# A fused attention and two-expert-layer kernel: first loads in a fixed order, and eight unread products ahead of the first round in place of eighteen in three places

## The chip, the core and the metric

The kernel runs on one core of a Trainium2 chip. The metric is the device time of one execution in microseconds (us). A core has a matrix engine (TensorE, PE in the rows), three engines for elementwise work (VectorE = DVE, ScalarE = ACT, GpSimd = POOL) and SyncE (SP), which here only issues DMA transfers. Each engine works through its own list of instructions; semaphores make one engine wait for another or for a transfer.

## The reference

Three stages follow each other on 2,304 tokens (4 batches of 576) with 512 channels:

```
q_p, k_p = exp(h - max h), h = x*scale @ omega.T - |x*scale|^2/2     # 8 heads of 64, 128 features
num = q_p @ (k_p.T @ v);  den = q_p @ sum(k_p) + 1e-6;  x = num/den   # linear attention
x = (silu(xn @ w_gate) * (xn @ w_val)) @ w_out                        # xn: RMS norm, 1536 wide
out = experts(x)   # 8 experts of 1024; each token goes to one, picked greedily, 288 tokens each
```

The weights of the middle stage are in float64 on the host and reach the kernel as pairs of 32-bit words.

## The kernel before, in words

**Attention** is a list of items: for batch 0 ten key items (head pair `p` 0 to 3, two or three groups `g` each), then eight query items, and so on for the other batches. An item's first step on PE is the projection (`proj_whole`, L393, tile `pp`); then DVE takes the maximum over the features (L397, `mx`) and ACT the exponential of four heads' columns (L400, `ft`, four instructions). One tick later PE multiplies the features of a key item with the values (L440, or L443 for the rest of a batch, tile `pm`). So in a tick PE runs the projection of one item and then the value products of the item before it; this is called a round below. `pp` has two buffers: a projection can start when ACT has read the `pp` of two items earlier.

**Weight units** run beside this. A unit loads 512 KB of word pairs into `ws` (L567, three buffers), ACT makes the magnitude (L572, tile `dw`), DVE the word (L576 to L578), ACT and GpSimd the split into two parts (L601, L602). The middle layer's products (L660 to L663, tile `gv`) enter PE's order from tick 23 and need these weights and the attention's output.

**Batch 1 and later** split their keys: ACT copies the high part (`split_k`, L365, `kh` from `kt`), GpSimd takes the low part (L366). The first such item comes after the eight query items of batch 0.

**What sets the order.** PE's order is written by hand (`manual_schedule` over the ticks). ACT, DVE, GpSimd and, before the change, SP get their order from a scheduler that works from its own picture of when each instruction is ready; whatever it decides is fixed in the program, and the engine then waits at each instruction in turn. Before the change, constants (`cf`, which holds the identity for the transposes, L779) were issued first of all by SP. A transfer on SP also waits until the transfer eight places earlier has landed, since eight semaphores (DMAHW0 to DMAHW7) are used in turn.

**Unread products.** `warm(n)` (L789) issues n products of a zeroed tile into a PSUM tile `lg` that nothing reads: 10 ahead of the first tick, 4 behind tick 0 and 4 behind tick 1.

Of the kernel before, what the change touches and what calls it, by code (L numbers as in the profile page):

```python
# [291 lines left out]
def kernel(ctx, tc, qT, kT, kC, v1, vC, om, wgv, rms, wo, woT, wg2, w1, w2, cfd, trd, cid, out, dbg=None):  # L292
    nc = tc.nc
# [10 lines left out]
    cf = keep.tile([128, C_N], F32, name="cf")  # L304
    ident = cf[:, C_ID:C_SL]
    cs = keep.tile([128, 1], F32, name="cs")
    gr = keep.tile([128, DM], F32, name="gr")
# [9 lines left out]
    wg2s = keep.tile([128, KD, E], F32, name="wg2s")  # L317
# [17 lines left out]
    def load_k(b, p):  # L335
        if b == 0:

            room = wpool.tile([128, 2, 1024], F32, name="wc")
            rooms[p] = room
            kt = room[:, 0, :512]  # L340
            vt = room[:, 1, :8 * (D + 1)].rearrange("p (t h d) -> p t h d", t=4, h=2)
        else:
            kt = kq.tile([128, 512], F32, name="kt", bufs=3)
            vt = kq.tile([128, 4, 2, D + 1], F32, name="vt", bufs=3)
        nc.sync.dma_start(kt, kT[b, p])
        nc.sync.dma_start(vt, v1[b, p])
        kts[b, p], vts[b, p] = kt, vt

    def load_c(b, r):
        if b == 0:  # L350
            kt = rooms[2 * r + 1][:, 0, 512:640]
            vt = rooms[2 * r + 1][:, 1, 520:520 + 4 * (D + 1)].rearrange("p (h d) -> p h d", h=2)
        else:
            kt = kq.tile([128, 128], F32, name="ktc", bufs=1)
            vt = kq.tile([128, 2, 2 * (D + 1)], F32, name="vtc", bufs=1)
        nc.sync.dma_start(kt, kC[b, r])
        nc.sync.dma_start(vt, vC[b, r])
        ktc[b, r], vtc[b, r] = kt, vt
# [10 lines left out]
    def load_q(c):  # L369
        if c < 4:  # L370
            if c == 0:
                st["qroom"] = wpool.tile([128, 4, 4, 128], F32, name="wc")
            qt = st["qroom"][:, c]
        else:
            qt = kq.tile([128, 4, 128], F32, name="qt")
        nc.sync.dma_start(qt, qT[c])
        qhs[c] = qt
# [377 lines left out]
    useq = [WgvUnit(f, g) for f in range(KF) for g in range(2)] + [WoTUnit(f) for f in range(KF)]  # L755
# [6 lines left out]
    nc.gpsimd.memset(idle.bitcast(F32), 0.0)  # L762
    ws = stage.tile([128, 2 * M], F32, name="ws")
    nc.scalar.dma_start(ws, om)
    load_k(0, 0)
    oms = wpool.tile([128, 2 * M], F32, name="wc")
    nc.scalar.mul(oms, ws, SCALE)
    nc.scalar.copy(omh, oms)
    nc.vector.tensor_sub(oml, oms, omh)
    load_k(0, 1)  # L770
    useq[0].load()
    load_k(0, 2)
    useq[1].load()
    load_c(0, 0)
    load_k(0, 3)
    load_c(0, 1)
    for c in range(2):
        load_q(c)
    nc.sync.dma_start(cf, cfd)  # L779
    useq[2].load()  # L780
    nc.sync.dma_start(gr, rms)
    for c in range(2, 4):
        load_q(c)
    nc.sync.dma_start(wg2s, wg2)
    nc.vector.memset(cs, -0.5)

    sink = psL.tile([128, 512], F32, name="lg")
# [1 line left out]
    def warm(n):  # L789
        for _ in range(n):  # L790
            nc.tensor.matmul(sink, idle[:, :128], idle[:, 128:], start=True, stop=True)
# [21 lines left out]
    def run_tick(tick):  # L813
        live = [(lag, items[tick - lag]) for lag in range(NLAG) if 0 <= tick - lag < len(items)]
        conv_pe(PACE[0] if tick < FFN_AT else PACE[1] if conv["next"] < 2 * KF else PACE[2])
        with tc.high_priority(offset=AHEAD_A):
            for lag, it in live:
                it.pe(lag)
        ffn_step_pe()
        for lag, it in live:  # L820
            if lag == 5 and isinstance(it, QItem) and it.hf and it.c * 128 // BLK not in xblk:
                while len(xblk) > 1:
                    ffn_step_el()
                    if not ffn_step_pe():
                        conv_el()
                        conv_pe(1)
        with tc.high_priority(offset=AHEAD_A):
            for lag, it in live:
                it.el(lag)
            if tick + 1 < len(items):  # L830
                items[tick + 1].split()
        ffn_step_el()
        conv_el()
        if tick + AHEAD < len(items):
            items[tick + AHEAD].load()
        if tick >= FFN_AT:
            conv["step"] += STEP - 1
            if conv["step"] >= 1:
                conv["step"] -= 1
                ffn_step_pe()  # L840
                ffn_step_el()

    with tc.manual_schedule(engines={mybir.EngineType.PE}):
        warm(10)
        for tick in range(len(items) + NLAG - 1):
            run_tick(tick)
            if tick < 2:
                warm(4)
    ac.close()


# [367 lines left out]
```

## Time and profile before

| | |
|---|---|
| median of 3 runs | 916.79 us (915.77 to 917.20) |
| the profiled execution | 915.83 us, span 914.0 us |
| PE busy | 898.2 us, 98% of the span |
| DVE busy | 553.6 us, 61% |
| ACT busy | 372.4 us, 41% |

The span runs from the first to the last instruction; 1.8 us of the execution's time lie around it. PE's busy time counts a matrix product from its start to a modelled end, so a busy PE is not a PE at its peak, and the shares are means over stages with different limits.

### The profile page before, as it was taken

Reading aid. Unit: us, or ns where it says so; the run is one execution under the profiler, and the core shown is the slowest. Engines: PE = TensorE matmul, PEld = TensorE weight load, DVE = VectorE, ACT = ScalarE, POOL = GpSimd, SP = SyncE. Lnnn points to the kernel's source line nnn. Section 1 sums busy time; section 2 is a strip of 40 time slices with the busy share of each in tenths; the row PEclk is TensorE's granted clock in tenths of the full one; section 3 lists DMA queues with packets and bytes.
Section 4 is the critical chain, followed back from the end, with each engine's and each line's share of the span. In section 5 each row is a group of like instructions: output and inputs, shape, how many; then the busy total and the mean of one; then the engine's idle time right before and its main releaser. Section 6 shows DMA issues by size and latency. Waiting matters only on the chain.

```text
span 914.0 us, 16175 instructions
## 1 busy us (share of the span) xinstructions
PE 898.2 (98%) x6171; PEld 781.0 (85%) x6171; DVE 553.6 (61%) x1262; ACT 372.4 (41%) x843; POOL 227.3 (25%) x298
## 2 busy tenths in 40 slices
PE   9999999999999999999999999999999999999996
PEld 8788888888888888777798777777789999999995
DVE  4898885656667765322273666666654665556561
ACT  6886565434544554332251110000014544454541
POOL 1354452222224332364241000000021122222111
PEclk9999999999999999999999999999999999999998
DMA  8656453454444642286583767766614656666650
GB/s 300 203 144 218 142 164 116 127 178 128 145 159 161 201 150 81 98 311 248 171 250 142 205 192 213 207 197 199 187 63 125 190 182 203 185 206 195 181 163 26
DMA packets 113213, 158.88 MB, mean 174 GB/s; under 512 B 6640, under 2 KB 70768, under 8 KB 113136
## 3 DMA queue, kind: packets, MB, share of 16 engines
q1 hardware_dynamic: 107328, 143.57, 50.5%
q0 software_dynamic: 3072, 9.44, 3.4%
q10 hardware_dynamic: 2736, 4.85, 1.4%
q8 instruction: 48, 0.79, 0.4%
q14 instruction: 29, 0.24, 0.1%
HBM read 113.79 MB, written 44.04 MB: 173 GB/s over the span
## 4 chain that ended last, share of the span: by engine, by line
PE 85%; issue 7%; DVE 4%; POOL 2%; ACT 2%; DMA 0%; POOLq 0%; ACTq 0%; DVEq 0%
PE py L973 16%; PE gv L660 11%; PE gv L661 10%; PE gv L663 10%; PE ph L1087 3%; PE ph L1084 3%; PE ph L1085 3%; PE py L1095 3%; PE py L1096 3%; PE py L1097 3%; PE pm L497 3%; PE pm L440 2%; PE cnt L181 2%; PE pm L486 1%; PE pp L388 1%
## 5 line engine op out<-in xcount | busy, mean ns | idle before, releaser
L660 PE MATMUL gv<-xh,wc 128*128 128x512 f32 (+1 forms) x480 | 180.0, 381 | 0.7 <-DVE th L673 0.7
L661 PE MATMUL gv<-xh,wc 128*128 128x512 f32 (+1 forms) x480 | 174.3, 370 | 0.0
L973 PE MATMUL py<-wc,ht 128*128 128x512 f32 x648 | 167.1, 404 | 0.0
L973 PEld LDWEIGHTS py<-wc,ht 128*128 128x128 f32 x648 | 114.9, 189 | 19.0
L663 PE MATMUL gv<-xl,wc 128*128 128x512 f32 (+1 forms) x480 | 118.4, 369 | 0.0
L660 PEld LDWEIGHTS gv<-xh,wc 128*128 128x128 f32 x480 | 90.6, 189 | 17.3 <-DVE th L673 1.7
L661 PEld LDWEIGHTS gv<-xh,wc 128*128 128x128 f32 x480 | 90.6, 189 | 13.8
L663 PEld LDWEIGHTS gv<-xl,wc 128*128 128x128 f32 x480 | 85.3, 189 | 15.8
L400 ACT ACTIVATE ft<-pp,mx 128x128 f32<-128x128 f32 x288 | 82.6, 373 | 27.7 <-DVE mx L397 25.0
L673 DVE SCALAR_TENSOR_TENSOR th<-th,gv 128x512 f32<-128x512 f32 (+1 forms) x60 | 37.9, 632 | 84.2 <-ACT th L672 84.2
L688 POOL TENSOR_TENSOR hp<-th,hp 128x512 fp32r<-128x512 f32 (+1 forms) x48 | 60.2, 1254 | 110.1 <-ACT hp L687 97.8
L944 DVE TENSOR_TENSOR wc<-ws,wc 128x512 fp32r<-128x512 f32 x128 | 84.8, 683 | 0.0
L1095 PE MATMUL py<-ehh,wc 128*128 128x288 f32 x256 | 77.7, 304 | 0.0
L1096 PE MATMUL py<-ehl,wc 128*128 128x288 f32 x256 | 75.9, 297 | 0.0
L1097 PE MATMUL py<-ehh,wc 128*128 128x288 f32 x256 | 75.8, 296 | 0.0
L1084 PE MATMUL ph<-exh,wc 128*128 128x288 f32 x256 | 71.6, 302 | 0.0
L1085 PE MATMUL ph<-exh,wc 128*128 128x288 f32 x256 | 69.8, 295 | 0.0
L984 ACT COPY ys<-py 128x512 f32<-128x512 f32 x18 | 10.6, 587 | 144.6 <-PE py L973 103.7
L954 ACT CAST wc<-ws 128x1024 fp32r<-128x1024 f32 x64 | 66.9, 1046 | 2.4 <-ACT ys L984 2.4
L397 DVE TENSOR_REDUCE mx<-pp 128x4 f32<-128x512 f32 (+1 forms) x76 | 50.0, 658 | 14.5 <-PE pp L393 8.1
L672 ACT ACTIVATE th<-gv 128x512 f32<-128x512 f32 (+1 forms) x60 | 33.2, 553 | 61.1 <-PE gv L663 53.3
L1089 DVE SCALAR_TENSOR_TENSOR ehl<-ph,ehh 128x288 fp32r<-128x288 f32 x64 | 29.3, 458 | 46.8 <-ACT ehh L1088 46.8
(214 smaller groups left out, 1714.2 us busy)
## 6 DMA issues: line engine op xcount, KB each, us to landing
ws<-in_w_dram SPq DMA_DIRECT2D x64, 512.0 KB, 4.2
ht<-h_dr SPq DMA_DIRECT2D x54, 512.0 KB, 4.2
h_dr<-hp SPq DMA_DIRECT2D x36, 512.0 KB, 2.8
ws<-in_wgv_dram SPq DMA_DIRECT2D x24, 512.0 KB, 4.3
h_dr<-hp SPq DMA_DIRECT2D x24, 256.0 KB, 2.7
ws<-in_woT_dram SPq DMA_DIRECT2D x12, 512.0 KB, 3.6
ws<-in_wo_dram SPq DMA_DIRECT2D x12, 512.0 KB, 3.8
h_dr<-ht SPq DMA_DIRECT2D x12, 512.0 KB, 3.2
```

The source lines that it names most:

```text
L400: st["ex"] = nc.scalar.activation(ft[:n, g], pp[:n, g], AF.Exp, bias=mx[:n, g:g + 1])
L660: nc.tensor.matmul(pg[:, :n], w[:, 0, v, k], xh[:, k, :n], start=(k == 0), stop=False)
L661: nc.tensor.matmul(pg[:, :n], w[:, 1, v, k], xh[:, k, :n], start=False, stop=False)
L663: nc.tensor.matmul(pg[:, :n], w[:, 0, v, k], xl[:, k, :n], start=False, stop=(k == KD - 1))
L944: nc.vector.tensor_sub(w[:, 1, h], sv[:, h], w[:, 0, h])
L954: nc.scalar.copy(w[:, 0], sv)
L973: nc.tensor.matmul(py, ht[:, i4, a], w[:, l, f % 2], start=(f == 0 and n == 0), stop=(f == KF - 1 and n == 2))
L1084: nc.tensor.matmul(ph, w[:, 0, k, m], xh[:, k], start=(k == 0), stop=False)
L1085: nc.tensor.matmul(ph, w[:, 1, k, m], xh[:, k], start=False, stop=False)
L1095: nc.tensor.matmul(py, w[:, 0, k], hh[:, k], start=(k == 0), stop=False)
L1096: nc.tensor.matmul(py, w[:, 0, k], hl[:, k], start=False, stop=False)
L1097: nc.tensor.matmul(py, w[:, 1, k], hh[:, k], start=False, stop=(k == KE - 1))
```

## The change

The first loads are written in one place, ahead of the preparation of omega, and a manual schedule over SP keeps them in that order: keys and values of head pairs 0 and 1, a weight unit, the rest of batch 0's keys for pairs 0 and 1, pair 2, a weight unit, pair 3 and its rest, two query blocks, then the constants, and so on. The unread products become 8 ahead of the first tick and none behind ticks 0 and 1.

```diff
     nc.scalar.dma_start(ws, om)
-    load_k(0, 0)
+    with tc.manual_schedule(engines={mybir.EngineType.SP}):
+        load_k(0, 0)
+        load_k(0, 1)
+        useq[0].load()
+        load_c(0, 0)
+        load_k(0, 2)
+        useq[1].load()
+        load_k(0, 3)
+        load_c(0, 1)
+        for c in range(2):
+            load_q(c)
+        nc.sync.dma_start(cf, cfd)
+        useq[2].load()
+        nc.sync.dma_start(gr, rms)
+        for c in range(2, 4):
+            load_q(c)
+        nc.sync.dma_start(wg2s, wg2)
     oms = wpool.tile([128, 2 * M], F32, name="wc")
...
-    load_k(0, 1)
-    useq[0].load()
-    load_k(0, 2)
-    useq[1].load()
-    load_c(0, 0)
-    load_k(0, 3)
-    load_c(0, 1)
...
-    nc.sync.dma_start(cf, cfd)
...
-        warm(10)
+        warm(8)
         for tick in range(len(items) + NLAG - 1):
             run_tick(tick)
-            if tick < 2:
-                warm(4)
```

The change moves instructions on SP, ACT, DVE and GpSimd, since the scheduler decides anew behind it. On SP, from the 14th load to the first loads of batch 1 (`kt`, `vt`), before; DMAHW names the semaphore of the transfer eight places earlier:

```order
L357 DMA wc_114<-in_vC_dram 128x260 [waits DMAHW3_49]
L345 DMA wc_126<-in_kT_dram 128x512 [waits DMAHW4_49]
...
L784 DMA wg2s_81<-in_wg2_dram 128x32 [waits DMAHW6_49]
L567 DMA ws_207<-in_wgv_dram 128x1024 [waits DMAHW7_49,DVE_49,Activation_49]
L567 DMA ws_242<-in_wgv_dram 128x1024 [waits DMAHW0_49,DVE_49,Activation_49]
L345 DMA kt_506<-in_kT_dram 128x512 [waits DMAHW1_49]
L567 DMA ws_280<-in_wgv_dram 128x1024 [waits DMAHW2_49,DVE_49,Activation_49]
```

The same place of SP's order in the changed kernel:

```order
L376 DMA wc_129<-in_qT_dram 128x512 [waits DMAHW7_49]
L376 DMA wc_129<-in_qT_dram 128x512 [waits DMAHW0_49]
L776 DMA cf_69<-in_cf_dram 128x339 [waits DMAHW1_49]
L567 DMA ws_133<-in_wgv_dram 128x1024 [waits DMAHW2_49,Activation_49]
L778 DMA gr_71<-in_rms_dram 128x512 [waits DMAHW3_49]
L376 DMA wc_129<-in_qT_dram 128x512 [waits DMAHW4_49]
L376 DMA wc_129<-in_qT_dram 128x512 [waits DMAHW5_49]
L781 DMA wg2s_81<-in_wg2_dram 128x32 [waits DMAHW6_49]
L345 DMA kt_499<-in_kT_dram 128x512 [waits DMAHW7_49]
L346 DMA vt_500<-in_v1_dram 128x520 [waits DMAHW0_49]
```

The first batch-1 key load (`kt_506` before, `kt_499` now) moved ahead of two weight units and stands directly behind `wg2s`; the 22 SP loads ahead of it are the same ones as the 22 that end with `wg2s` before.

On ACT, the third and fourth items of attention before (`ft_199`, `ft_218`), which the unit's magnitude (`dw`) precedes:

```order
L572 ACTIVATE dw_184<-ws_117 128x512 [waits DMAHW4_49]
L400 ACTIVATE ft_199<-pp_190,mx_197 128x128 [waits DVE_49]
L400 ACTIVATE ft_199<-pp_190,mx_197 128x128 x3
L400 ACTIVATE ft_218<-pp_209,mx_216 128x128 [waits DVE_49,Activation_49]
L400 ACTIVATE ft_218<-pp_209,mx_216 128x128 x3
L400 ACTIVATE ft_236<-pp_228,mx_234 128x128 [waits DVE_49]
```

And in the changed kernel (`ft_192`, `ft_211`):

```order
L572 ACTIVATE dw_181<-ws_115 128x512 [waits DMAHW5_49]
L400 ACTIVATE ft_192<-pp_183,mx_190 128x128 [waits DVE_49]
L400 ACTIVATE ft_192<-pp_183,mx_190 128x128 x3
L365 CAST kh_576<-kt_499 128x256 [waits DMAHW7_49]
L365 CAST kh_631<-kt_499 128x256
L400 ACTIVATE ft_211<-pp_202,mx_209 128x128 [waits DVE_49,Activation_49]
L400 ACTIVATE ft_211<-pp_202,mx_209 128x128 x2
L400 ACTIVATE ft_229<-pp_221,mx_227 128x128 [waits DVE_49]
```

Two copies of batch 1's keys (L365, from `kt_499`) now stand between the third and the fourth item; before, they stand behind the second query block's first copy.

On PE, the first rounds before:

```order
L791 MATMUL lg_142<-wc_103 128x512 x9
L393 MATMUL pp_155<-wc_110,wc_107 128x256 [waits DMAHW2_49,Activation_49]
L393 MATMUL pp_155<-wc_110,wc_107 128x256
L791 MATMUL lg_142<-wc_103 128x512 x4
L393 MATMUL pp_169<-wc_110,wc_107 128x256 x2
L440 MATMUL pm_172<-wc_107,ft_160 128x65 [waits DMAHW3_49,Activation_49]
L440 MATMUL pm_172<-wc_107,ft_160 128x65 [waits Activation_49] x3
L791 MATMUL lg_142<-wc_103 128x512 x4
```

And in the changed kernel, through the value products of the fourth item:

```order
L792 MATMUL lg_145<-wc_103 128x512 x7
L393 MATMUL pp_156<-wc_140,wc_109 128x256 [waits DMAHW1_49,Activation_49]
L393 MATMUL pp_156<-wc_140,wc_109 128x256
L393 MATMUL pp_166<-wc_140,wc_109 128x256 x2
...
L393 MATMUL pp_221<-wc_140,wc_112 128x256 [waits DMAHW6_49,DVE_49]
L440 MATMUL pm_169<-wc_112,ft_211 128x65 [waits Activation_49] x4
L393 MATMUL pp_237<-wc_140,wc_119 128x256 [waits DMAHW0_49,DVE_49]
```

The groups of four are gone, and the rest of PE's order is as before: behind the fifth item's projection (`pp_221`) PE waits at `pm_169<-ft_211` for ACT.

## Rows read from the trace of the kernel before

**Rows 1.** The page: span, and each engine's busy time.

```profile
span 914.0 us, 16175 instructions
PE 898.2 (98%) x6171; PEld 781.0 (85%) x6171; DVE 553.6 (61%) x1262; ACT 372.4 (41%) x843; POOL 227.3 (25%) x298
```

**Rows 2.** Windows: stretch, its length, engines' busy us, granted clock, DMA share, GB/s.

```profile
13.50:25.00 11.50, 11.50 (x74) 9.96 (x73) 7.70 (x14) 10.27 (x31) 2.54 (x2) 1.00 0.81 278
25.00:40.00 15.00, 14.22 (x89) 11.27 (x88) 12.37 (x27) 13.07 (x41) 5.98 (x7) 1.00 0.84 261
40.00:60.00 20.00, 17.97 (x135) 16.47 (x135) 17.95 (x36) 18.36 (x55) 10.28 (x14) 1.00 0.38 113
60.00:75.00 15.00, 14.31 (x84) 12.23 (x83) 14.79 (x21) 10.19 (x26) 9.18 (x8) 1.00 0.71 216
75.00:100.00 25.00, 25.00 (x144) 21.74 (x143) 20.38 (x42) 13.85 (x34) 10.04 (x10) 1.00 0.59 175
```

**Rows 3.** Chain that ended last, 0 to 80 us: start, us, what.

```profile
1.43 4.14 PE lg L791 x10
5.57 0.86 PE pp L393 x4
6.43 0.93 PE lg L791 x4
...
9.07 0.98 PE lg L791 x4
10.05 0.87 PE pp L393 x4
10.92 0.84 PE pm L440 x8
...
70.00 0.70 DVE dw L577
```

**Rows 4.** Timeline of ACT and DVE: start, us, what, idle time before it and releaser.

```profile
3.88 0.42 ACT L767 ACTIVATE wc<-ws 128x256 f32<-128x256 f32 x1 [1.41 <-DMA ws<-in_om_dram]
6.47 0.69 DVE L397 TENSOR_REDUCE mx<-pp 128x4 f32<-128x512 f32 x1 [1.28 <-PE pp L393]
8.99 1.14 ACT L400 ACTIVATE ft<-pp,mx 128x128 f32<-128x128 f32 x4 [0.66 <-DVE mx L397]
10.01 0.68 ACT L572 ACTIVATE dw<-ws 128x512 f32<-128x512 f32 x1
13.50 1.69 ACT L400 ACTIVATE ft<-pp,mx 128x128 f32<-128x128 f32 x6 [0.62 <-DVE mx L397]
31.13 0.74 ACT L365 CAST kh<-kt 128x256 fp32r<-128x256 f32 x2
```

**Rows 5.** Timeline of SP's issues, 0 to 20 us.

```profile
1.19 0.42 SPq L345 DMA_DIRECT2D wc<-in_kT_dram  x1
...
2.13 0.43 SPq L567 DMA_DIRECT2D ws<-in_wgv_dram  x1
...
15.13 0.66 SPq L784 DMA_DIRECT2D wg2s<-in_wg_dram  x1
15.90 3.75 SPq L567 DMA_DIRECT2D ws<-in_wgv_dram  x2
```

**Rows 6.** DMA view, windows of rows 5's issues: size, us to landing.

```profile
wc<-in_kT_dram SPq DMA_DIRECT2D x1, 256.0 KB, 3.2
ws<-in_wgv_dram SPq DMA_DIRECT2D x1, 512.0 KB, 6.7
wg2s<-in_wg_dram SPq DMA_DIRECT2D x1, 16.0 KB, 6.4
```

**Rows 7.** DMA view, 0 to 40 us: GB/s in each us.

```profile
GB/s 0 34 224 389 195 185 330 352 398 429 390 393 360 344 261 317 332 311 358 421 260 274 336 119 33 74 233 267 386 141 205 403 248 263 259 230 344 413 352 94
```

**Rows 8.** Windows at the end of the execution, columns as in rows 2.

```profile
904.50:905.00 0.50, 0.50 (x5) 0.29 (x3) 0.14 (x1) 0.03 (x1) 0.00 (x0) 1.00 0.00 0
905.00:909.00 4.00, 0.04 (x1) 0.00 (x0) 1.28 (x4) 0.61 (x2) 2.67 (x5) 1.00 0.28 77
909.00:910.00 1.00, 0.00 (x0) 0.00 (x0) 0.00 (x0) 0.00 (x0) 0.26 (x1) 0.69 0.49 152
910.00:911.00 1.00, 0.00 (x0) 0.00 (x0) 0.00 (x0) 0.00 (x0) 0.00 (x0) 0.50 0.42 131
```

More of the change, by code (lines that the diff above doesn't have):

```diff
@@ L769 @@
     nc.vector.tensor_sub(oml, oms, omh)
-    load_k(0, 1)
-    useq[0].load()
-    load_k(0, 2)
-    useq[1].load()
-    load_c(0, 0)
-    load_k(0, 3)
-    load_c(0, 1)
-    for c in range(2):
-        load_q(c)
-    nc.sync.dma_start(cf, cfd)
[L780 to L784, printed above, removed]
     nc.vector.memset(cs, -0.5)
```

## The prediction, made blind

> **What bounds the kernel now.** I read the page first: PE is busy for 98% of the span [rows 1], but that share hides the start. The chain of waits tells it apart [rows 3]: up to about 24 us it runs over PE alone, round after round, with the unread products in it; after that it changes between ACT, DVE and PE, and at 70 us it still runs over DVE, on the weight units. From 75 us PE is busy in every microsecond [rows 2]. So what the change is worth is decided before 75 us: PE then has a backlog to the end, and a delay (or gain) of ACT and DVE in that stretch is handed on whole. The windows show that little slack is left there: ACT is busy for 10.27 of 11.5 us, 13.07 of 15 and 18.36 of 20 up to 60 us, and DVE for 17.95 of 20 and 14.79 of 15 from 40 to 75 us [rows 2].
>
> **The part that is meant: the unread products.** At the start ten took 4.14 us, 0.41 each; the later groups of four took 0.93 and 0.98, 0.23 to 0.25 each [rows 3]. [...] With eight, the row ends at 1.43 + 8 x 0.41 = 4.7 us. The first projection needs scaled omega, ready at 3.88 + 0.42 = 4.3 us [rows 4], and the first keys, landed at 1.19 + 3.2 = 4.4 us [rows 5, 6] behind the constants, which no longer stand ahead of them. So it starts near 4.8 instead of 5.57 us, 0.8 us earlier. The second projection follows at once (0.86 us each [rows 3]), and the maximum (0.69) and four exponentials (1.14) of item 1 [rows 4] end at 4.8 + 0.86 + 0.69 + 1.14 + 0.1 for the hand-overs = 7.6 us. The value products of item 1 and then the third projection come at about 7.8 us, where before it began at 10.05 [rows 3]: 2.2 us earlier.
>
> **Why this gain isn't kept.** ACT's order in the changed kernel has, behind the third item's exponentials, two copies of batch 1's keys (L365) that read `kt_499`. Nobody needs them for fourteen more items, but ACT takes its list in turn: before, it sat 1.41 us ahead of its first scaling for a transfer while there was nothing else it could do [rows 4]. [...]
>
> *When do they start?* `kt_499` is the 23rd load on SP and stands right behind `wg2s`. The 22 SP loads ahead of it are those of before in another order, so the same bytes have to pass. Before, the last of these was issued at 15.13 us and landed 6.4 us later, at 21.5; the 512 KB behind it were issued at 15.90 and landed 6.7 us later, at 22.6 [rows 5, 6]. Half as many bytes, 256 KB, land about half-way: 21.5 + 1.1/2 = 22.05 us. The earliest bound comes from the rates: summed over the first 21.5 us, 6.4 MB had moved [rows 7]; at the best rate of a single microsecond, 429 GB/s, held from the 2nd on, that takes 15 us, so 17 us. The latest is that of a full unit, 22.6. Nothing in the rows supports 17: the rate fell to 185 and 195 at 4 to 6 us and to 261 at 14 us. I take 22.0.
>
> *What stands still.* ACT reaches the copies at about 11 us: the unit's magnitude, which precedes item 3's exponentials, needs a 512 KB load that landed at 2.13 + 6.7 = 8.8 us before [rows 5, 6] and now has one more pair of keys and values ahead of it, though no constants (I take 9.3); 0.68 for the magnitude and 1.14 for the exponentials [rows 4] make 11.1. From there ACT waits until 22.0. PE does the fourth and fifth projections and then waits in its order at the value products of item 4; DVE waits for the sixth projection, GpSimd for the low parts of the same keys. All compute engines stand, for some 10 us.
>
> *The price.* Before, item 4's exponentials began at 13.50 us [rows 4]. Now they begin when the load has landed and the two copies (0.74 us [rows 4]) are done: 22.05 + 0.74 = 22.8 us. **Term 1: +9.3 us** (bounds 17 + 0.74 - 13.5 = 4.2 and 22.6 + 0.74 - 13.5 = 9.8).
>
> **The clock after the stall.** At the end of the execution the last product is over by 905.1 us; the granted clock averages 1.00 until 909, 0.69 in the next microsecond and 0.50 from 910 on [rows 8]: a PE left without products falls to the lower level. [...] A round takes 0.87 + 0.84 = 1.71 us on PE at the upper level [rows 3], so about 3.4 at the lower, while ACT, with 1.14 for the exponentials and 0.68 for a unit's step [rows 4], needs about 1.8 a round: then PE is the slower one, by 1.6 us a round. [...] **Term 2: +1.6 us**; below, 0 (the clock doesn't fall, or ACT's backlog hides it); above, half of 4.14, 2.1. [...]
>
> **What comes back.** The two copies are done and are missing at 31.13 us, where ACT has little idle time: **term 3: -0.7 us**. All loads of batch 0 have landed when work resumes, but the rounds before 24 us were no longer held up by loads either: the chain there is PE [rows 3]. Loads for the next weight units are now queued behind seven loads of batch 1; the first of them is issued once `wg2s` has landed, at 21.5, and with the 6 to 7 us of the loads above lands by 28, while ACT asks for it four exponential groups and some four unit steps after 22.8, near 30. This costs nothing, and would cost two or three microseconds if it took ten. PE's order is otherwise untouched, ACT and DVE fall back into their old order within the first 75 us.
>
> **Sum.** 9.3 + 1.6 - 0.7 = +10.2 us. Against the profiled execution (span 914.0 and 1.8 around it, 915.83) that is 926.0; the median of the runs shown is 0.96 above that execution, which would give 927.0. I put 926.5. A change of less than 0.2% (1.8 us) counts as none, about what a measurement of this kernel can tell.
>
> **The rivals.**
>
> *The stall is partly made up.* Same stall, but with all data present ACT and DVE run more densely up to 60 us. The most that ACT's idle time there can give is 1.2 + 1.9 + 1.6 = 4.7 us [rows 2], so +10.2 - 4.7 = +5.5, 922. For it: everything is in SBUF. Against: the order is fixed, and much of that idle is one engine waiting for another, not for loads. Chance 0.15.
>
> *The clock stays low longer.* [...] Chance 0.13.
>
> *The load comes in time.* The gain of 2.2 us is kept and the time is 914.6 if `kt_499` has landed when ACT gets to it, at 11.1 us; the change stays a gain as long as it lands before about 13.5 - 0.7 = 12.8. For it: its place moved ahead of two units. Against: by 12.8 us only 3.6 of the 6 MB and more had moved before [rows 7]. Chance 0.03.
>
> *No measurable change.* The load lands at its 17 us bound, term 2 is nothing, and the stretch to 60 us takes back three or four microseconds. Chance 0.02.
>
> **Chances.** The forecast itself, a stall of nine to eleven microseconds that is handed on, has 0.67; its own range is 924 to 929, from term 1 between 8 and 9.8 and term 2 between 0 and 2.1 plus the distance to the median. Slower by over 0.2%: 0.67 + 0.15 + 0.13 = 0.95; same 0.02; faster 0.03. The range of eight in ten goes from 921 (nearly the whole of the made-up case) to 930 (the long cold stretch).
>
> **What the changed profile would show.** ACT's `kh` copy (L365) with an idle time of about 10 us ahead of it, released by the load into `kt`, at 22 us; PE's third projection near 8 us instead of 10, then PE idle until about 23; a granted clock of 0.50 inside that gap and shortly behind it; DVE's weight work and the start of steady matrix products (75 us before) some ten microseconds later, and no differences in length behind that. The prediction is wrong if the copies find their load landed, if the clock stays up through the gap (1.6 less), or if steady work starts less than eight microseconds later.

## The result and the profile after

The changed kernel takes 927.93 us (median of 5 runs, 926.11 to 928.58), the kernel before in the same session 917.20 (915.77 to 918.89): ratio 1.0114, 95% interval 1.0102 to 1.0126. That is 10.7 us more, inside the range and 1.4 us above the forecast. The profiled execution after took 928.58 us.

The page of the changed kernel, span and busy times [rows 1 for before]:

```profile
span 926.8 us, 16153 instructions
PE 900.1 (97%) x6161; PEld 782.8 (84%) x6161; DVE 556.9 (60%) x1262; ACT 373.2 (40%) x843; POOL 225.9 (24%) x298
```

The engines do what they did: PE's busy time differs by 1.9 us, the span by 12.8 (1.6 of it is a stretch at a lower clock, 0.66 for 5 us, that this execution has and the one before doesn't, see the last section). Most of the rest is time in which PE ran nothing, 8.84 us in one wait, and the page can't say where. The timeline of ACT can (start, length, what, idle time before it and who ended it):

```profile
4.42 0.42 ACT L783 ACTIVATE wc<-ws 128x256 f32<-128x256 f32 x1 [1.95 <-DMA ws<-in_om_dram]
...
9.61 0.67 ACT L572 ACTIVATE dw<-ws 128x512 f32<-128x512 f32 x1 [0.21 <-DMA ws<-in_wgv_dram]
10.61 1.14 ACT L400 ACTIVATE ft<-pp,mx 128x128 f32<-128x128 f32 x4 [0.32 <-DVE mx L397]
20.67 0.71 ACT L365 CAST kh<-kt 128x256 fp32r<-128x256 f32 x2 [8.93 <-DMA kt<-in_kT_dram]
21.29 1.65 ACT L400 ACTIVATE ft<-pp,mx 128x128 f32<-128x128 f32 x6
...
26.39 0.38 ACT L454 COPY kvs<-pm 128x260 f32<-128x260 f32 x1 [2.38 <-PE pm L443]
26.66 1.14 ACT L400 ACTIVATE ft<-pp,mx 128x128 f32<-128x128 f32 x4
```

The two copies of batch 1's keys stand at 20.67 us behind 8.93 us of waiting. Item 4's exponentials follow at 21.29, where before they began at 13.50 [rows 4]: 7.79 us later. The chain that ended last shows the same stretch as transfers on SP, then the key load, then the copies (start, length, what):

```profile
2.12 6.04 DMA wc<-in_v_dram
8.18 6.00 DMA wc<-in_v_dram
14.19 0.33 SPq L376
...
15.51 5.14 DMA kt<-in_kT_dram
...
20.98 0.40 ACT kh L365
...
21.70 1.97 PE pm L440 x8
23.67 1.81 PE pp L393 x4
```

The two value loads are the 4th and the 12th load of SP, the query load issued at 14.19 is the 20th: each waited for the one eight places earlier (landed at 8.16, issued at 8.18; landed at 14.18, issued at 14.19). The key load, the 23rd, went out three issues later. So its landing is the end of three transfers of 5 to 6 us, one behind the other.

Before, PE's rows of this kind were 0.84 and 0.87 long [rows 3]; behind the gap they take 1.97 and 1.81. The windows give the reason in the column after the busy times, the granted clock:

```profile
13.00:20.00 7.00, 0.00 (x0) 0.00 (x0) 0.99 (x2) 0.00 (x0) 0.00 (x0) 0.72 1.01 353
20.00:24.00 4.00, 2.30 (x10) 2.21 (x10) 0.00 (x0) 3.33 (x10) 1.89 (x3) 0.50 1.06 360
24.00:26.00 2.00, 2.00 (x8) 1.73 (x7) 0.42 (x1) 0.01 (x1) 0.79 (x1) 0.50 0.86 332
26.00:28.00 2.00, 2.00 (x13) 1.72 (x13) 1.97 (x5) 1.61 (x6) 0.00 (x0) 0.92 0.37 142
```

From 13 to 20 us PE, ACT and GpSimd do nothing at all while the transfers run at full share (1.01). The waits of the first 30 us name who stands behind whom (engine, line, releaser; us in total, times, longest):

```profile
POOL kl L366 <- ACT kh L365: 19.8, 1, 19.8
DVE mx L397 <- issue: 11.6, 1, 11.6
...
PE pm L440 <- ACT ft L400: 9.2, 2, 8.8
ACT kh L365 <- DMA kt<-in_kT_dram: 8.9, 1, 8.9
```

For DVE's wait the view names no releaser ("issue"); DVE's next maximum is that of item 6, whose projection stands behind PE's waiting value products and ends at 25.48 on the chain. So one wait for a transfer has become a wait of all four engines. Further on PE is busy without a gap, as before from 75 us on [rows 2], so the delay was handed on:

```profile
75.00:85.00 10.00, 10.00 (x59) 8.74 (x58) 8.68 (x13) 5.63 (x16) 5.21 (x6) 1.00 0.81 238
```

### The profile page after: what moved, and what is told of

It is laid out like the page before. It is cut to its first block, busy times and chain, and to the rows that moved or that the text cites. A ratio compares the mean times of both kernels' runs of the same rounds, so it can differ in the third digit from the quotient of the medians.

```text
span 926.8 us, 16153 instructions
## 1 busy us (share of the span) xinstructions
PE 900.1 (97%) x6161; PEld 782.8 (84%) x6161; DVE 556.9 (60%) x1262; ACT 373.2 (40%) x843; POOL 225.9 (24%) x298
## 4 chain that ended last, share of the span: by engine, by line
PE 85%; issue 6%; DVE 4%; DMA 2%; POOL 1%; ACT 0%; SPq 0%; POOLq 0%; ACTq 0%; DVEq 0%
PE py L972 16%; PE gv L660 11%; PE gv L661 10%; PE gv L663 10%; PE pm L497 3%; PE ph L1086 3%; PE ph L1083 3%; PE ph L1084 3%; PE py L1094 3%; PE py L1095 3%; PE py L1096 3%; PE pm L440 2%; PE cnt L181 2%; PE pm L486 2%; PE pp L388 1%
## 5 line engine op out<-in xcount | busy, mean ns | idle before, releaser
L688 POOL TENSOR_TENSOR hp<-th,hp 128x512 fp32r<-128x512 f32 (+1 forms) x48 | 58.0, 1208 | 114.6 <-ACT hp L687 106.8
L687 ACT CAST hp<-th 128x512 fp32r<-128x512 f32 (+1 forms) x48 | 27.1, 566 | 77.3 <-DVE th L685 77.3
```

## The experiments

To place a delay, one row is followed through all kernels below: the group of four exponentials that begins at 133.68 us in the profiled execution of the kernel before, 144.33 in the changed one:

```profile
133.68 1.15 ACT L400 ACTIVATE ft<-pp,mx 128x128 f32<-128x128 f32 x4
144.33 1.15 ACT L400 ACTIVATE ft<-pp,mx 128x128 f32<-128x128 f32 x4
```

Its distance to 133.68 is called the shift; the table at the end of this section has all of them. The theory of the prediction (A) is that the loss is the time at which the load lands that ACT's hoisted copies wait for. The rivals are that the missing products and PE's clock make it (B), or that the new load order costs by itself, wherever ACT's copies stand (C); below, a second cost (U) joins them.

### The products alone

The kernel before with eight products ahead of the first tick and none between:

```diff
-        warm(10)
+        warm(8)
...
-            if tick < 2:
-                warm(4)
```

> The kernel before with 8 unread products ahead of the first tick and none behind ticks 0 and 1; the loads as before. Theory A: no copy of batch 1's keys moves ahead, so no stall; the third projection waits for keys that land at 9.4 us, so the gain is small: 0.5 us, 0 to 1.5 us faster, ratio 0.998 to 1.000. Theory B: the loss of the changed kernel, 6 to 11 us. Theory C: as theory A.

Measured: 916.90 us against 916.98, ratio 1.0002 (0.9991 to 1.0013). Eighteen unread products or eight are the same to this kernel. B as the cause of the loss falls, and so does the view that the products held the kernel up in a way that counts: item 4's exponentials begin at 13.32 instead of 13.50 us. (The shift, read from one execution, is 0.88 here although the medians agree: shifts that differ by less than about 1 us say little.)

### The loads alone

The changed kernel with the products of before (10, 4 and 4).

> The changed kernel with the 18 unread products of before (10, 4 and 4). The order of ACT has the two copies one item earlier here, ahead of the third item's exponentials. Theory A: the copies wait until the load lands at 20.7 us, the third item follows at about 21.4 instead of 11.74 us, 9.6 later, and the clock adds 2: 11 to 13 us above the kernel before, 928 to 930 us, a little worse than the changed kernel although the products are back. Theory B: about the time of the kernel before, 917 us. Theory C: 3 us or more above.

Measured: 929.80 us, ratio 1.0148 (1.0130 to 1.0165). The whole loss is there without the change in the products, and a little more. In ACT's timeline the scheduler put the copies one item earlier, ahead of item 3's exponentials:

```profile
19.10 0.71 ACT L365 CAST kh<-kt 128x256 fp32r<-128x256 f32 x2 [7.26 <-DMA kt<-in_kT_dram]
19.72 2.17 ACT L400 ACTIVATE ft<-pp,mx 128x128 f32<-128x128 f32 x8
```

The copies come 1.57 us earlier than in the changed kernel, and still item 6's exponentials come 10.77 us late (27.64 us) in place of 9.79. One more round stands behind the gap, since item 3's exponentials, too, come behind the copies: the windows from 20 to 26 us have 24 matrix products at a granted clock of 0.50, and the one from 26 to 30 is at 0.78. The changed kernel has 18 at 0.50 up to 26 us, and item 3's value products were done before its gap.

### The copies taken out of the way

All key copies of batch 1 and later are tied behind the exponential that is the latest one in program order:

```diff
-        nc.scalar.copy(kh[:, :n], src)
+        with tc.issue_after(st["ex"].ins):
+            nc.scalar.copy(kh[:, :n], src)
```

> The changed kernel with one addition: the copies of the later batches' keys (L365 and L366 of the changed kernel) are tied behind the exponentials that precede them in the program, so that none stands between the third and the fourth item. Theory A (these copies, waiting for the first batch-1 key load, make the whole loss): no idle time of 8.9 us on ACT; the fourth item's exponentials begin at about 12.3 us, 1.2 us before the kernel before (13.50); ratio to the kernel before 0.996 to 1.001, some 1 to 2 us faster than before and 11 us faster than the changed kernel. Theory B (taking out the unread products lets the clock fall and that makes the loss): still 6 us or more above the kernel before, with a granted clock of 0.50 in the first 30 us. Theory C (the fixed load order itself is late somewhere): 3 us or more above the kernel before, with an idle time released by another load.

Measured: 938.88 us, ratio 1.0246 (1.0230 to 1.0261): far slower than the changed kernel, against A's number. The profile shows that A's step was right and that two others came behind it. ACT's timeline no longer has the wait at 12 us; item 4's exponentials begin at 11.94, 1.56 us ahead of before. Then ACT waits for a weight unit:

```profile
11.94 0.88 ACT L401 ACTIVATE ft<-pp,mx 128x128 f32<-128x128 f32 x3 [0.62 <-DVE mx L398]
...
25.69 0.66 ACT L573 ACTIVATE dw<-ws 128x512 f32<-128x512 f32 x1 [4.84 <-DMA ws<-in_wgv_dram]
```

SP's timeline has that unit's load at 20.02, behind seven loads of batch 1, of which the first went out at 14.91:

```profile
14.91 0.52 SPq L345 DMA_DIRECT2D kt<-in_kT_dram  x1
...
20.02 0.36 SPq L568 DMA_DIRECT2D ws<-in_wgv_dram  x1
```

And from 40 to 90 us the tied copies are late for PE (`PE pp L389 <- ACT kh L366`, 6.9 us in 5 waits), the clock column falling to 0.91 and 0.67 in the windows of 40 to 60 and 60 to 85 us. The run mixes a cure with two costs, one of them from this edit itself. It raises theory U: the loads queued ahead of the units cost by themselves, and the stall had hidden it.

### The gap filled with products

The changed kernel with 34 unread products behind tick 3, where PE would stand:

```diff
             run_tick(tick)
+            if tick == 3:
+                warm(34)
```

> The changed kernel with 34 further unread products placed in PE's order behind tick 3, where PE stands anyway until ACT's copies are done: at 0.23 us each they fill some 7.9 of the 8.8 us. It prices the clock alone. If the clock's fall makes term 2: the granted clock stays at 1.00 through 30 us, the sixth item's exponentials begin 7.7 to 8 us later than before instead of 9.8, and the time is 2 us less than that of the changed kernel, 925.5 to 926.5. If the rounds behind the stall are late for another reason (ACT's backlog, the units): the time stays at 927 to 928.5.

Measured: 927.80 us, ratio 1.0122 (1.0106 to 1.0137), the same as the changed kernel. The windows show the gap full and the clock up, and PE's timeline shows the first value products behind it in 1.21 us (1.97 without the filling):

```profile
13.00:20.00 7.00, 7.00 (x33) 5.67 (x31) 0.00 (x0) 0.00 (x0) 0.00 (x0) 1.00 1.04 380
20.00:24.00 4.00, 2.74 (x17) 2.03 (x15) 1.06 (x2) 3.35 (x10) 2.57 (x3) 1.00 0.98 314
```

```profile
21.53 1.21 PE L440 MATMUL pm<-wc,ft 128*128 128x65 f32 x8 [1.26 <-ACT ft L400]
```

The stall itself is as long as in the changed kernel (9.09 us ahead of the copies). By the time alone the second branch of the expectation holds. Against what the expectation says, though, the run doesn't price the clock alone: behind the gap the scheduler changed the order of ACT and DVE too. Two steps of weight units (L601, L572) now stand ahead of item 5's two exponentials:

```profile
21.12 1.14 ACT L400 ACTIVATE ft<-pp,mx 128x128 f32<-128x128 f32 x4
22.13 0.63 ACT L601 CAST wc<-dw 128x512 fp32r<-128x512 f32 x1
22.64 0.70 ACT L572 ACTIVATE dw<-ws 128x512 f32<-128x512 f32 x1
23.21 0.64 ACT L400 ACTIVATE ft<-pp,mx 128x128 f32<-128x128 f32 x2
24.43 0.38 ACT L454 COPY kvs<-pm 128x260 f32<-128x260 f32 x1 [0.58 <-PE pm L443]
25.81 1.14 ACT L400 ACTIVATE ft<-pp,mx 128x128 f32<-128x128 f32 x4 [1.00 <-DVE mx L397]
```

and on DVE two steps of a unit (L576, L577, from 23.37) stand ahead of item 6's maximum (25.03), which in the changed kernel comes first (25.58). From item 4's exponentials to the copy L454 it takes 3.31 us here, 5.10 in the changed kernel and 3.03 before: up to there the clock is worth some 1.8 us. One row on, at item 6, ACT waits 1.00 us for the late maximum and only 0.7 of the 1.8 is left. The shift is 9.86 us instead of 10.65, and 0.17 of that stood at item 4 already. So this kernel gains by the clock and loses by its order; what the low clock costs the whole run stays open.

### The key load in another place

The changed kernel with batch 1's first keys and values as fifth and sixth load of SP. The scheduler then puts the copies at the head of ACT's list, ahead of the scaling of omega.

```diff
-            if self.b and self.g == 0:
+            if self.b and self.g == 0 and (self.b, self.p) not in kts:
...
         load_k(0, 1)
+        load_k(1, 0)
         useq[0].load()
```

> The changed kernel with one edit: the first keys and values of batch 1 are loaded right after the keys of the second head pair, as fifth and sixth load of SP. ACT's two copies of these keys then stand at the head of its queue, ahead of the scaling of omega. Theory A (the loss is the landing time of the load that ACT's copies wait for): the load is issued near 2.6 us and lands near 7, so ACT starts its work near 7.8 instead of 4.42, the first projections move by 3.3 us, no wait of 8.9 us near 13 to 21 us is left, and the time falls to 919 to 922. Theory C (the loss is that 1 MB and more of batch 1 goes ahead of the weight units, wherever ACT stands): the same bytes still go ahead of the units, and the time stays at 926 to 929.

Measured: 920.57 us, ratio 1.0044 (1.0028 to 1.0059), in A's range. ACT's timeline: the wait is still there, at another time, with the length that the landing gives it. The load was issued at 2.60 us.

```profile
7.45 0.71 ACT L365 CAST kh<-kt 128x256 fp32r<-128x256 f32 x2 [4.98 <-DMA kt<-in_kT_dram]
8.06 0.41 ACT L784 ACTIVATE wc<-ws 128x256 f32<-128x256 f32 x1
```

The scaling of omega, at 4.42 in the changed kernel, is at 8.06, 3.64 us later, and the shift is 4.39 in place of 10.65. The order of the first loads is the changed one but for this pair; C as the cause of the loss, which put 926 to 929, falls.

### Copies late, loads late, both

Three kernels take the two placements apart. In the first, the two copies of batch 1's first keys are tied behind the eleventh group of exponentials (they come at row 38 of ACT's list, 12 in the changed kernel, 43 before). In the second, batch 1's loads are tied behind those of weight units 4 to 7 (counted from 0, so from the fifth unit on), where the kernel before has them. The third does both. `exs` collects the exponentials, `ld` is a unit's load.

```diff
         def load(self):
+            late = {(1, 0): 4, (1, 1): 5, (1, 2): 6, (1, 3): 7}.get((self.b, self.p))
+            with tc.issue_after(useq[late].ld.ins) if late else ExitStack():
...
         def split(self):
+            late = exs[10] if (self.b, self.p) == (1, 0) else None
+            with tc.issue_after(late.ins) if late else ExitStack():
...
```

> The changed kernel with the two copies of batch 1's first keys tied behind the eleventh group of exponentials, so that they stand on ACT where the kernel before has them within a few instructions (row 38 for row 43); the loads keep the changed order, seven loads of batch 1 ahead of the fourth weight unit's. In the first of these runs, with every such copy tied, ACT waited 4.84 us for a weight unit. Theory U (the loads queued ahead of the units cost by themselves what the stall had hidden): no wait at the copies, then 4 to 6 us of waiting for the load of the fourth unit near 20 to 26 us, and 919.5 to 923. Theory N (these loads cost nothing, as the prediction had it): 915 to 916.5, at or just under the kernel before.

> The changed kernel with the loads of batch 1's four head pairs tied behind those of weight units 4, 5, 6 and 7 (counted from 0), which puts them in SP's queue where the kernel before has them; nothing is said of the copies, which the scheduler puts at row 33 of ACT (row 12 in the changed kernel, 43 in the kernel before). Theory A: the first of these loads is issued near 19 and lands near 24 us, ACT comes to row 33 near 21.5, waits some 2 us and copies for 0.7: 917 to 920. Theory C or any cost of the new first loads themselves: 922 or more.

> Both ties: loads of batch 1 behind units 4 to 7 and the first two copies behind the eleventh group of exponentials. New first loads and eight products stay. Theory A with U: neither wait is left, 915 to 917, between 0.2% faster and no change, since the early gain near 1 us of the new order may stay. If something else in the new first loads costs (their order, the eight products): 918 or more.

Measured, against 916.61 us for the kernel before: copies late 922.75 (ratio 1.0065, 1.0053 to 1.0077), loads late 918.02 (1.0013, 1.0002 to 1.0023), both 918.03 (1.0020, 1.0011 to 1.0029).

*Copies late* differs from the changed kernel, up to the fourth unit's load, by the place of two instructions (0.71 us together) and gives 4 to 5 us back. What remains is U, as expected there: nothing at 12 us, and then the fourth unit's load, issued at 20.65 behind seven loads of batch 1, keeps ACT for 4.57 us. Its timeline:

```profile
20.31 1.17 ACT L400 ACTIVATE ft<-pp,mx 128x128 f32<-128x128 f32 x4
26.04 0.66 ACT L575 ACTIVATE dw<-ws 128x512 f32<-128x512 f32 x1 [4.57 <-DMA ws<-in_wgv_dram]
...
33.50 0.73 ACT L365 CAST kh<-kt 128x256 fp32r<-128x256 f32 x2
```

*Loads late* alone removes the first wait and most of the second: the copies stand at row 33, ACT reaches them at 24.77 us with no wait (I had put 2 us), and the fourth unit costs 1.05 instead of 4.57. Its timeline:

```profile
22.20 0.66 ACT L574 ACTIVATE dw<-ws 128x512 f32<-128x512 f32 x1 [1.05 <-DMA ws<-in_wgv_dram]
...
23.27 1.65 ACT L400 ACTIVATE ft<-pp,mx 128x128 f32<-128x128 f32 x6
24.77 0.74 ACT L365 CAST kh<-kt 128x256 fp32r<-128x256 f32 x2
```

*Both late* is no better: 1 us above what A and U together gave, in the branch of a further cost (918 or more). Its timeline has the copies at 27.87 without a wait, and this ahead of them:

```profile
19.82 1.17 ACT L400 ACTIVATE ft<-pp,mx 128x128 f32<-128x128 f32 x4
22.41 0.66 ACT L577 ACTIVATE dw<-ws 128x512 f32<-128x512 f32 x1 [1.42 <-DMA ws<-in_wgv_dram]
...
23.48 1.65 ACT L400 ACTIVATE ft<-pp,mx 128x128 f32<-128x128 f32 x6
```

Up to there it runs 0.46 us ahead of the kernel before (exponentials at 19.82 for 20.28), behind it 1.36 us late (23.48 for 22.12). Two query loads of 256 KB each, which went out ahead of the fourth unit's, were the next suspects.

### Query loads late as well

Both ties, and the loads of query chunks 4 and 5 tied behind the seventh unit's:

```diff
         def load(self):
-            if self.hf == 0 and self.c > 3:
-                load_q(self.c)
+            late = useq[6] if self.c in (4, 5) else None
+            with tc.issue_after(late.ld.ins) if late else ExitStack():
+                if self.hf == 0 and self.c > 3:
+                    load_q(self.c)
```

> The kernel with both ties (loads of batch 1 behind units 4 to 7, first two copies behind the eleventh group of exponentials) and a third: the two query loads of chunks 4 and 5, which there went out at 14.68 us ahead of the fourth unit's load, are tied behind the seventh unit's, where the kernel before has them. With both ties alone ACT still waited 1.42 us for the fourth unit's load at 22.41 and ran 1.49 us behind the kernel before from there on. If that wait is the whole of what is left (theory A with U carried on): the load goes out about 1 us earlier with 0.5 MB less ahead of it, the wait is gone, the early gain of 0.5 to 1 us stays, 915 to 916.8, that is from 0.2% faster to no change against the kernel before. If the new first loads or the eight products cost something of their own: 917.5 to 918.5, as with both ties.

Measured: 917.84 us against 916.57, ratio 1.0010 (1.0000 to 1.0019). The wait for the unit is gone, the median is not better, and lies in the expectation's second branch (a cost of the new first loads or the products of their own, 917.5 to 918.5):

```profile
20.99 0.68 ACT L579 ACTIVATE dw<-ws 128x512 f32<-128x512 f32 x1
22.18 0.62 ACT L608 CAST wc<-dw 128x512 fp32r<-128x512 f32 x1 [0.52 <-DVE dw L585]
22.79 1.66 ACT L400 ACTIVATE ft<-pp,mx 128x128 f32<-128x128 f32 x6
```

ACT now waits for DVE at this place: the scheduler has one more unit step (L608) ahead of the exponentials of items 9 and 10, which come at 22.79 for 22.12 before. The profiled execution also has a short stretch at a lower clock (a mean of 0.98 from 120 to 180 us, last section). With the products alone measuring nothing, what is left, about 1 us, points at the new order; no run takes it apart further. No kernel here is measurably faster than the kernel before.

### The runs side by side

The shift is worked out as the start of the group named above less 133.68.

| kernel | median us | before, same runs | ratio | shift us |
|---|---|---|---|---|
| changed | 927.93 | 917.20 | 1.0114 | 10.65 |
| products alone | 916.90 | 916.98 | 1.0002 | 0.88 |
| loads alone | 929.80 | 916.98 | 1.0148 | 11.67 |
| all copies tied | 938.88 | 916.98 | 1.0246 | 21.33 |
| gap filled | 927.80 | 916.98 | 1.0122 | 9.86 |
| key load early | 920.57 | 916.61 | 1.0044 | 4.39 |
| copies late | 922.75 | 916.61 | 1.0065 | 6.57 |
| loads late | 918.02 | 916.61 | 1.0013 | 1.49 |
| both late | 918.03 | 916.61 | 1.0020 | 1.49 |
| both and queries late | 917.84 | 916.57 | 1.0010 | 1.12 |

## Why the prediction was right

**The step that decides held.** ACT, in its order, waited 8.93 us for a load that nothing near it needed; item 4's exponentials stood behind the copies until 21.29 us although their maximum was done at 12.26. Every engine stood behind ACT, and the delay was handed on whole. *Copies late* shows that this place is the cause: the same loads in the same order up to the fourth unit's, with two instructions further down ACT's list, cost 6.1 us over the kernel before instead of 10.7 (by the shift, 6.57 instead of 10.65). *Key load early* shows that the landing time sets the price.

**Term 1, +9.3: measured +7.8.** The load landed at 20.65 us instead of 22.05. It was issued at 15.51 and took 5.14 us; I had put its landing half a microsecond behind that of `wg2s` before, 21.5, which had been 6.4 us under way. And the exponentials began 0.62 us after the copies did, not 0.74. On the chain the landing is that of three transfers eight places apart, a way of counting that the prediction didn't use; the DMA share was about 1 meanwhile (1.01 from 13 to 20 us), so the bytes and the places can't be told apart here.

**Term 2, +1.6: right in size for the place; what of it reaches the end is open.** From item 4 to item 6 (16.87 us before, 26.66 after) the delay grew from 7.79 to 9.79, by 2.0. PE's two rows above, 1.97 and 1.81 us at a granted clock of 0.50, are the doubled round, and they lie on the chain there. The kernel with the gap filled had 1.8 us of this back at the copy before item 6, but its other order on ACT and DVE took most of it again, so its median, equal to the changed kernel's, doesn't show that the clock costs nothing. That the term counts one round at the low clock, and half of the first 4.14 us at most, was the author's estimate, which no run shows: the clock column is at 1.00 over those ten products. In its place the changed kernel showed 0.54 from 16 to 17 us, in the gap, 0.50 from 17 to 26, 0.92 from 26 to 28 and 1.00 from 28 to 30.

**Term 3, -0.7: not seen.** From item 6 to the row at 133.68 the delay grew by another 0.86 us where a gain of 0.7 was expected. In the kernel with all three ties, which waits for no unit load up to there, the exponentials of items 9 and 10 still come 0.67 us late and the shift is 1.12, so some of this may belong to ACT's new order of unit steps rather than to the stall. No run changes that order alone, and a shift of 0.88 us is what the products alone have without a change in time.

**The meant gain** was swallowed, as forecast. The third projection began at 8.70 us, 1.35 earlier instead of 2.2. The first one began at 5.01 instead of 4.8 (scaled omega came at 4.84, not 4.3), and its first two products took 0.67 and 0.57 us, for 0.38 of the later ones, with the clock column at 1.00; the prediction counted 0.86 us for all four. Without the stall the lead is 0.8 to 1.5 us at item 4 and is gone by item 9: *both late* and *both and queries late* end at no gain. So the rival that had the load come in time, 914.6, was also too good: it counted on a lead that the next 10 us use up.

**What was wrong: "This costs nothing".** The prediction said that the weight units' loads, queued behind seven loads of batch 1, are hidden. In the changed kernel they are, since ACT itself is 8 us late. Take that away and they cost 4.57 us at the fourth unit and 5.1 by the row at 133.68 (6.57 with the copies late, 1.49 with the loads late too). Both costs start from one thing: the manual schedule on SP ends with `wg2s`, and directly behind it the scheduler put seven loads of batch 1, ahead of the fourth unit. The copies follow the place of their load: row 12 of ACT here, the head of the list with the load in fifth place, row 33 with the load behind a unit's, each time without a tie on the copies. That the scheduler believed the load landed is inferred from this. *Loads late* undoes this alone and brings the time from 927.9 to 918.0, nearly all of the loss.

**The sum**, 10.2, was right by errors that cancel: -1.5 in term 1, +0.4 in term 2, +1.6 where term 3 stood; 9.3 + 1.6 - 0.7 became 7.8 + 2.0 + 0.9 = 10.7. The mechanism was right; that the sum came so close was partly luck.

## What to carry to other kernels

When part of a queue is fixed by hand, look at what the scheduler does directly behind the fixed part: here what moved there, not the fixed part, made the loss. Where an engine takes its list in turn, as ACT did here for 8.93 us, an instruction that reads a transfer must not be hoisted by a guess of when it lands; tie the load or the reader to work near its first use, and one place at a time: tying every reader, as in *all copies tied*, cost more than it cured, while tying the loads repaired nearly all. And a cost that seems hidden is hidden by something: ask what it becomes when that is repaired, or a cure will show the next wait instead of a gain.

## What the runs showed of the hardware

Besides the stall's, there is a second low stretch of the clock while PE has work. In the profiled execution of the changed kernel the windows are:

```profile
183.00:186.00 3.00, 2.25 (x19) 1.83 (x17) 1.78 (x5) 0.60 (x1) 0.00 (x0) 1.00 0.71 197
186.00:191.00 5.00, 5.00 (x21) 4.17 (x20) 0.86 (x2) 2.09 (x6) 0.73 (x1) 0.66 0.42 144
```

PE is busy for all of 186 to 191 us at a mean clock of 0.66, behind a pause of 0.75 us. The pause alone doesn't decide it. The kernel before has one of 0.8 us ahead of the same matrix product (`gv` from `wg2s`), at a clock of 1.00 in the windows from 160 to 200 us. In seven more kernels PE's busy time in that part, 120 to 200 us, is 0.75 us short as well. In five of the nine the mean clock is below 1.00 there: 0.91 from 180 to 200 us in the changed one, gap filled and copies late, 0.93 from 160 to 180 and 0.98 from 180 to 200 in loads late, 0.98 from 120 to 180 and 0.99 from 180 to 200 in both and queries late. In the other four (before, products alone, key load early, both late) it is 1.00. What the stretch costs can be read from ACT: the last four exponentials begin at 359.80 us before and at 372.04 in the changed kernel, so a delay of 10.65 at the row followed above has become 12.24, 1.6 more. By the spans, from that row to the end the delay grows by 1.3 to 2.2 us in the five kernels, and by -0.3 to 0.5 in products alone, key load early and both late.

Executions of one kernel differ in the clock too: the five of the changed kernel have means of 0.989 (928.58 and 928.50 us) or 0.992 (926.11 to 927.93), the kernel before 0.998 at 915.11 and 0.993 at 918.79. If a stretch of 1.6 us is behind this, a difference of up to 0.2% between two medians here can come from it alone; that is an estimate, 1.6 of 917 us. What decides it stays open.
